# Row maxima kept in PSUM, bias and mask of the first pairs as matmuls, and another order of the pair run, in a fused attention and gated feed-forward kernel

## The chip, the cores and the metric

The kernel runs on one core of a Trainium2 chip. The metric is the device time of one execution in microseconds (us), as the median of several timed runs. Beside the timed runs one execution was taken by the hardware profiler; all rows below come from it.

## The reference

```python
# q, k, v: (8 batches, 8 heads, 576, 64); s: (8, 8, 576)
scores = (1 / sqrt(64)) * q @ k.T
cum    = cumsum(maximum(s, 0), axis=-1)
scores = where(causal, -1e9, scores + minimum(-(cum[:, None] - cum[None, :]), 0))
attn   = exp(scores - max(scores))
attn   = attn / (attn.sum() + 1e-9)
x      = attn @ v                      # heads side by side: (8, 576, 512)
h      = maximum(x @ w_in, 0)          # w_in: (512, 1024), in fp64
conv   = sum(conv_w[k] * h_shifted_by(k - 1) for k in 0, 1, 2)   # along the sequence
out    = (h * sigmoid(conv)) @ w_out   # w_out: (1024, 512), in fp64
```

## The kernel before

Attention runs over 32 pairs: pair p holds two heads, one on partitions 0 to 63 and one on 64 to 127 (the two lanes, j = 0 and 1), with the head dimension on the partitions. Four pairs make a batch. After a batch's four pairs the second layer of that batch follows: `h` (x by w_in), the convolution and the gate, and `o` (u by w_out).

**One pair.** Its keys and queries are loaded (`raw`), and split into a high and a low part for fp32 accuracy (L1014, L1018). The row maxima are needed before the exponential, so TensorE first multiplies the high parts alone, with queries on the partitions: the shift matmuls (L1085, task `sh`). They come in four parts (SH_PARTS): 288 keys of the last query block; its other 288; 448 of block 3 and 64 of block 0; 320 of block 2 and 192 of block 1. Each part takes two PSUM banks, one per lane, and a bank is free again when VectorE has read its maximum. That is L1102, `tensor_tensor_reduce`: it adds to the PSUM block a row of the scaled cumulated bias (`bb`, loaded with the same row on all partitions by a 576 KB DMA, L1045, and masked on the diagonal block by GpSimd's `affine_select`, L1058) and takes the maximum along the row into one column of `r`. It must also write the sum somewhere; here that is one bf16 scrap tile in SBUF, `junk`. On VectorE it shows as two instructions, CUSTOM_DVE_ANT_0 and DVE_READ_ACCUMULATOR2_ANT. A pair has 12 of them.

The maxima are turned (a TensorE transpose, L1126), copied by ScalarE with a base value added (L1134), and sent by DMA into two rows of `eq` (the shift rows, L1142). The score matmuls (L1174, task `sc`), keys on the partitions, are again four parts of two banks: per block three products of high and low parts, and one of `ek` by `eq`, which adds the bias and the shift. `ek` holds nine rows per lane of the bias, loaded by L1028: for pairs 0 and 1 straight from the SBUF tile `bx`, later from a copy in DRAM (`rows_d`). For pairs 0 to 7 the causal mask is added by a bf16 matmul of `unit` and `mask` (L1178); from pair 8 on GpSimd cuts the result (L1209). ScalarE takes the exponential (L1196). Then TensorE adds up rows (L1252, `sum`) and multiplies by the values (L1234, `pv`). The row sums go through a guard, a reciprocal, DRAM and back as `rb`, and the normalization (L1298) and a split (L1313, L1317) give `x`.

**PSUM.** Two of the eight banks hold `pv`; six are handed out to the shift parts, the scores, the sums and the second layer.

**What sets the order.** All work is cut into tasks with the engines on which they may run and an estimated duration. A planner, `Sched.play`, simulates the engines when the kernel is built, and each engine takes, of the tasks that are ready, the one with the smallest due time. Due times stand in a table of numbers, DUE. One rule goes beyond them: from pair 8 (B0) on, the sums and values of the pair before, the scores of this pair and the shift parts of the next form a pair run: on TensorE they follow each other in the fixed order ORDER, with nothing between. All engines then execute their instructions in the order thus found; what waits for another engine waits on its semaphore.

**Weights.** w_in, w_out and conv_w come in fp64 and are put together to fp32 by bit operations on VectorE (L866, L877, L880, L888, tasks `one`, `two`, `three`), a piece at a time. The convolution's two outer taps are two `scalar_tensor_tensor` in one task (L1386).

## Time and profile before

| | before |
|---|---|
| timed runs, median of 3 | 818.46 us (818.03 to 819.22) |
| the profiled execution | 821.87 us |
| its span | 820.2 us |
| TensorE (PE), matmuls | 8437 |
| VectorE (DVE), instructions | 1367 |
| ScalarE (ACT) busy | 437.3 us |
| GpSimd (POOL) busy | 370.9 us |
| DMA | 82.32 MB, mean 100 GB/s |

PE is TensorE's matmuls, PEld its weight loads, which lie beside them; DVE is VectorE, ACT ScalarE, POOL GpSimd, SP SyncE, whose queue (SPq) issues the DMAs. In a row of a timeline the two numbers in front are start and duration in us; a bracket at its end gives the time that the engine stood idle before it and what ended that. "x6" stands for six instructions in one row, which overlap and of which the row gives the whole stretch. PEclk is the granted TensorE clock as a share of the full 2.4 GHz. The stretches in the last section are cut at events: 48.58 us is the start of the first row sums, 111.78 us that of the first matmul of the second layer, 184 us about that of the first pair run, 733 us the end of the last.

### The profile page before, as it was taken

What the parts mean: (1) busy time and instruction counts of PE and PEld (TensorE: products, weight loads), DVE (VectorE), ACT (ScalarE), POOL (GpSimd) and SP (SyncE); (2) the same over time, 40 slices, a digit from 0 to 9 for tenths busy, and PEclk for the clock granted to TensorE, in tenths of its full rate; (3) what the DMA queues carried; (4) which work ended last, traced back from release to release, by engine and by line L of the source; (5) the groups of instructions that cost most, each with busy time, mean ns of one, the idle gap of its engine ahead of it and who ended that gap; (6) DMA issues with size and microseconds to landing.
All of it is one profiled execution on the core that took longest, in us unless ns stands there. A gap on an engine that the chain in (4) does not pass through costs nothing.

```text
span 820.2 us, 21742 instructions
## 1 busy us (share of the span) xinstructions
PE 769.1 (94%) x8437; PEld 685.5 (84%) x8437; DVE 539.6 (66%) x1367; ACT 437.3 (53%) x998; POOL 370.9 (45%) x633
## 2 busy tenths in 40 slices
PE   1498999999999999999999999999899999999998
PEld 1266677898989889898988989898798989899998
DVE  6878989876585756657576655656586566754633
ACT  5345556764573546546564547545454666454543
POOL 8237443355455254636454454546426362513122
PEclk9999999999999999999999999999999999999999
DMA  7836534423314132333223142333303320111001
GB/s 244 272 122 189 159 114 147 154 82 112 102 51 143 55 118 81 110 104 104 88 80 114 64 134 84 103 110 83 111 35 110 109 81 16 51 43 52 16 30 37
DMA packets 59004, 82.32 MB, mean 100 GB/s; under 512 B 6617, under 2 KB 39705, under 8 KB 58841
## 3 DMA queue, kind: packets, MB, share of 16 engines
q1 hardware_dynamic: 58901, 80.94, 31.5%
q8 instruction: 66, 1.08, 0.6%
q14 instruction: 37, 0.30, 0.1%
HBM read 67.48 MB, written 13.19 MB: 98 GB/s over the span
## 4 chain that ended last, share of the span: by engine, by line
PE 72%; DVE 12%; issue 5%; ACT 5%; DMA 3%; POOL 1%; SPq 1%; DVEq 0%; POOLq 0%; ACTq 0%
PE ps L1444 23%; PE ps L1349 21%; PE ps L1174 12%; PE pv L1234 7%; DVE junk L1102 5%; PE ps L1252 4%; DVE ct L1386 3%; PE ps L1085 3%; ACT pt L1196 2%; DVE ct L1405 1%; DMA ek<-bx 1%; DMA raw<-qk 1%; DMA rb<-ri_d 1%; PE ps L1178 1%; DMA w<-w_in 1%
## 5 line engine op out<-in xcount | busy, mean ns | idle before, releaser
L1444 PE MATMUL ps<-u,wo 128*128 128x288 f32 x1536 | 218.3, 298 | 0.5 <-ACT ob L1461 0.5
L1349 PE MATMUL ps<-x,wi 128*128 128x290 f32 x1536 | 215.7, 298 | 0.4 <-ACT pt L1196 0.4
L1349 PEld LDWEIGHTS ps<-x,wi 128*128 128x128 f32 x1536 | 209.2, 190 | 1.6 <-ACT pt L1196 0.6
L1444 PEld LDWEIGHTS ps<-u,wo 128*128 128x128 f32 x1536 | 208.0, 189 | 2.5 <-ACT ob L1461 0.7
L1386 DVE SCALAR_TENSOR_TENSOR ct<-ht,cw_sb,ct 128x288 f32<-128x288 f32 (+1 forms) x256 | 150.0, 589 | 90.0 <-ACT ct L1372 84.5
L1196 ACT ACTIVATE pt<-ps,bias_sb 128x288 f32<-128x288 f32 (+4 forms) x384 | 153.4, 477 | 85.2 <-PE ps L1174 84.7
L1416 POOL TENSOR_TENSOR u<-ct,u 128x576 fp32r<-128x576 f32 x64 | 96.4, 1509 | 212.6 <-ACT u L1412 176.3
L1102 DVE CUSTOM_DVE_ANT_0 junk<-ps,bb 128x64 bf16<-128x64 f32 (+4 forms) x320 | 137.1, 429 | 67.3 <-PE ps L1085 26.7
L1058 POOL TENSOR_SCALAR_AFFINE_SELECT bb<-bb 128x128 f32<-128x128 f32 (+1 forms) x256 | 90.3, 360 | 137.0 <-DVE r L1102 120.5
L1174 PE MATMUL ps<-s 64*128 64x288 f32 (+4 forms) x1152 | 126.5, 316 | 9.1 <-ACT pt L1196 4.3
L1174 PEld LDWEIGHTS ps<-s 64*128 64x128 f32 x1152 | 97.4, 190 | 22.8 <-ACT pt L1196 10.5
L1209 POOL TENSOR_SCALAR_AFFINE_SELECT pt<-pt 128x128 f32<-128x128 f32 (+1 forms) x240 | 79.9, 349 | 48.7 <-ACT pt L1196 47.3
L1360 ACT ACTIVATE ht<-ps 128x289 f32<-128x289 f32 x128 | 52.7, 412 | 84.0 <-PE ps L1349 82.9
L1234 PE MATMUL pv<-pt,v 128*32 128x448 f32 (+4 forms) x1536 | 97.3, 396 | 0.0
L1018 POOL TENSOR_TENSOR s<-raw,s 128x1152 fp32r<-128x1152 f32 x31 | 83.1, 2680 | 23.4 <-DVE s L1014 15.3
L1234 PEld LDWEIGHTS pv<-pt,v 128*32 128x32 f32 x1536 | 63.0, 112 | 29.1 <-issue 24.2
L1085 PE MATMUL ps<-s 64*128 64x288 f32 (+4 forms) x384 | 52.9, 340 | 21.0 <-ACT s L1014 7.9
L1174 PE MATMUL ps<-eq,ek 64*128 64x288 f32 (+4 forms) x384 | 69.2, 322 | 0.9 <-DMA eq<-rt 0.9
L1372 ACT ACTIVATE ct<-ht,cw_sb 128x288 f32<-128x288 f32 x122 | 65.4, 536 | 5.0
L1252 PE MATMUL ps<-pt,onehot 128*32 128x144 f32 (+4 forms) x1792 | 63.8, 278 | 2.1 <-DVE r L1102 1.3
L1252 PEld LDWEIGHTS ps<-pt,onehot 128*32 128x32 f32 x1792 | 56.9, 115 | 9.2 <-issue 3.6
L1085 PEld LDWEIGHTS ps<-s 64*128 64x128 f32 x384 | 33.0, 194 | 36.8 <-DVE r L1102 9.0
(82 smaller groups left out, 594.2 us busy)
## 6 DMA issues: line engine op xcount, KB each, us to landing
raw<-qk SPq DMA_DIRECT2D x32, 576.0 KB
bb<-cum_d SPq DMA_DIRECT2D x32, 576.0 KB
v<-vp SPq DMA_DIRECT2D x32, 320.0 KB
rb<-ri_d SPq DMA_DIRECT2D x64, 144.0 KB
outT<-ob SPq DMA_DIRECT2D x64, 144.0 KB
ht<-w_out SPq DMA_DIRECT2D x16, 256.0 KB
w<-w_in SPq DMA_DIRECT2D x8, 512.0 KB
ri_d<-ri SPq DMA_DIRECT2D x32, 72.0 KB
```

The costliest lines, as they stand in the source:

```text
L1018: tt_on(e)(st[:, 0:2, :], R_t[raw.slot], st[:, 2:4, :].bitcast(F32), op=ALU.subtract)
L1058: nc.gpsimd.affine_select(out=dst, in_=src, pattern=[[0, n], [-1, P if tau else P - PAD]], compare_op=ALU.is_ge, fill=NEG, base=0 if tau e ...
L1085: nc.tensor.matmul(dst[j], l, S_t[sb.slot][r, 2, c0:c1], start=True, stop=True)
L1102: nc.vector.tensor_tensor_reduce(out=junk[:, 0 : c1 - c0], in0=bank(pb, o, o + c1 - c0), in1=in1, scale=1.0, scalar=acc if c0 else -3.0e38 ...
L1174: nc.tensor.matmul(dst[j], l, m, start=(k == 0), stop=(k == 3))
L1196: nc.scalar.activation(PT_t[pts[j].slot][0:jt, O_T[t] + c0 : O_T[t] + c1], bank(pb, o, o + c1 - c0)[0:jt], AF.Sigmoid, bias=bias_sb[0:jt, ...
L1234: nc.tensor.matmul(pvt[gs, o0 : o0 + c1 - c0], vt[0:jt, t, gs], PT_t[pts[g // 2].slot][0:jt, O_T[t] + c0 : O_T[t] + c1], start=(t == 0), s ...
L1252: nc.tensor.matmul(bank(sb_, o0, o0 + b_ - a_)[32 * g : 32 * g + 32], onehot[:, j, :], src[:, a_ - c0 : b_ - c0], start=t == 0 and j == 0, ...
L1349: nc.tensor.matmul(bank(hb, 0, XW), l, r, start=(k == 0), stop=(k == len(seq) - 1))
L1386: nc.vector.scalar_tensor_tensor(cc[:, lo:hi], h_[:, sh + lo : sh + hi], cw_sb[:, 3 * f + k : 3 * f + k + 1], cc[:, lo:hi], op0=ALU.mult, ...
L1416: tt_on(e)(uu[:, 1], C_t[ct.slot], uu[:, 0].bitcast(F32), op=ALU.subtract)
L1444: nc.tensor.matmul(bank(pb, 0, HS), l, r, start=(fp == 0 and k == 0), stop=(fp == NF // 2 - 1 and k == len(seq) - 1),)
```

## The change

- The maxima write the biased block back into the PSUM bank they read (`out=src`) instead of `junk`, and stand in an order that alternates the two lanes. One `affine_select` cuts the `bb` of both lanes.
- For pairs 0 to 5 (B1) the bias is added on TensorE: behind each shift matmul stands one of indicator rows EB by `ek`, and the diagonal blocks but the last get the mask by a matmul of `unit` and `mask` (three blocks wide now). VectorE then takes a plain maximum (`tensor_reduce`) where a row block begins at key 0, ten a pair, and keeps the old form with `mask` as the added tile for the second half of the last block. These pairs load no `bb` and have no cuts; their shift matmuls now need `ek`; their turned maxima are copied by one instruction.
- ORDER is changed, the two taps and the two ORs of a weight piece become tasks of their own, SW replaces the number 0.19 in the planner, and DUE is new throughout.
- On SyncE's queue six `bb` loads go, and the second `bb` load (pair 7's) now stands between the `ek` loads of pairs 0 and 1.

```diff
+B1 = 6
...
+SW = 0.12
...
-ORDER = ("sh0", "sh1", "sh2", "sum", "pv", "sc0", "sh3", "sc1", "sc2", "sc3")
+ORDER = ("sh0", "sum", "pv", "sh1", "sc0", "sh2", "sc1", "sc2", "sh3", "sc3")
...
 DUE = (
-    -114439, -2886, -5304, -2876, -2883, -2878, -5567, -4957, -5119, -16050, -13717, 193, -603,
+    -71591, -3748, -2936, -3146, -2870, -3586, -4314, -2902, -3422, -2825, -6319, -11723, -11558,
...
-                        dur += 0.19
+                        dur += SW
...
-    MW = 2 * P
+    MW = 3 * P
-    junk = const.tile([P, P * (NT - 1) - PAD], BF16, name="junk")
+    EB_t = const.tile([P, FW], F32R, name="eb")
...
+    t_eb = add("eb", [("ACT", 0.72)], [t_masks], -188, c_ind(EB_t))
...
                 nc.vector.scalar_tensor_tensor(
                     wb, wd[:, :, 1], 0xC0000000, wb, op0=ALU.bitwise_and, op1=ALU.bitwise_or
                 )
+
+            def low(e):
+                wd, _, wb = parts()
                 nc.vector.scalar_tensor_tensor(
                     wb, wd[:, :, 0], 29, wb, op0=ALU.logical_shift_right, op1=ALU.bitwise_or
                 )
...
-        last_v[0] = t_v = add(f"v{p}", [("SP", 0.4)], [last_v[0], *t_ind], A - 2, load_v,
+        last_v[0] = t_v = add(f"v{p}", [("SP", 0.4)], [last_v[0], t_eb, *t_ind], A - 2, load_v,
...
-        bb = buf("bb")
+        early = p < B1
+        if not early:
...
+        if not early:
+            t_bb = add(f"bb{p}", [("SP", 0.4)], [t_cum_d], a_sh - BBA, load_bb, alloc=[bb],
+                       nbytes=2 * P * S * 4)
+
+        def cut(tau, deps):
             def run(e):
-                b_ = BB_t[bb.slot][:, j0 : j0 + n]
+                b_ = BB_t[bb.slot]
                 c0 = P * tau - PAD
                 src = b_[:, :, max(c0, 0) : c0 + P]
                 dst = b_[:, :, S : S + P - PAD] if tau == 0 else src
                 nc.gpsimd.affine_select(
-                    out=dst, in_=src, pattern=[[0, n], [-1, P if tau else P - PAD]],
+                    out=dst, in_=src, pattern=[[0, 2], [-1, P if tau else P - PAD]],
                     compare_op=ALU.is_ge, fill=NEG, base=0 if tau else -PAD, channel_multiplier=1,
                 )
 
-            return add(f"{name}{p}.{tau}.{j0}", [("POOL", 0.18 + n * 0.135, True)], deps, a_sh - 1.0,
-                       run, uses=[bb])
-
-        cuts = {}
-        for tau in (L, 0):
-            t_cut = cut("cu", [0, 1], tau, [t_bb])
-            cuts[tau, 0] = cuts[tau, 1] = t_cut
-
+            return add(f"cu{p}.{tau}", [("POOL", 0.42 if tau else 0.3, True)], deps, a_sh - 1.0, run,
+                       uses=[bb])
+
+        cuts = {} if early else {tau: cut(tau, [t_bb]) for tau in (L, 0)}
 
         r8, rt = buf("r8"), buf("rt")
         maxima, last_mx = [], {}
...
                         l = S_t[sb.slot].rearrange("p a c -> p (a c)")[
                             r, 3 * S - PAD + P * tau : 3 * S - PAD + P * tau + P]
                         nc.tensor.matmul(
-                            dst[j], l, S_t[sb.slot][r, 2, c0:c1], start=True, stop=True
+                            dst[j], l, S_t[sb.slot][r, 2, c0:c1], start=True, stop=not early
                         )
+                    if early and tau < L:
+                        dg = min(P, c1)
+                        for j in range(2):
+                            nc.tensor.matmul(
+                                dst[j][:, c1 - dg : c1], unit, mask[:, MW - dg : MW],
+                                start=False, stop=False,
+                            )
+                    if early:
+                        for j, r in enumerate(lanes):
+                            nc.tensor.matmul(
+                                dst[j], EB_t[r, P * tau : P * tau + P],
+                                EK_t[ek.slot][r, c0:c1], start=False, stop=True,
+                            )
                     o += c1 - c0
 
             w = sum(c1 - c0 for _, c0, c1 in part)
-            t_mm = add(f"sh{p}.{i}", [("PE", sum(c_rt(c1 - c0) for _, c0, c1 in part))], [t_hi],
+            t_mm = add(f"sh{p}.{i}", [("PE", (1 + early) * sum(c_rt(c1 - c0) for _, c0, c1 in part)
+                                           + 0.22 * early * sum(tau < L for tau, _, _ in part))],
+                       [t_hi] + ([t_dr, t_eb, t_ident] if early else []),
                        a_sh + 0.1 * i, sh_mm, alloc=pbs + ([r8] if i == 0 else []),
-                       uses=[sb], mode="r", prev=None if p - 1 >= B0 else t_mm,
+                       uses=[sb] + ([ek] if early else []), mode="r", prev=None if p - 1 >= B0 else t_mm,
                        burst=group(p - 1, f"sh{i}"))
             note(p - 1, f"sh{i}", t_mm, [t_hi])
-            for j in range(2):
-                o = 0
-                for tau, c0, c1 in part:
+            o = 0
+            for tau, c0, c1 in part:
+                for j in range(2):
+                    w = c1 - c0
+
                     def sh_max(e, j=j, tau=tau, c0=c0, c1=c1, o=o, pb=pbs[j]):
                         acc = R8_t[r8.slot][:, j * NT + tau : j * NT + tau + 1]
-                        in1 = BB_t[bb.slot][:, j, c0:c1] if tau else BB_t[bb.slot][:, j, S : S + c1]
+                        src = bank(pb, o, o + c1 - c0)
+                        if early and not c0:
+                            nc.vector.tensor_reduce(
+                                out=acc, in_=src, axis=mybir.AxisListType.X, op=ALU.max
+                            )
+                            return
+                        if early:
+                            in1 = mask[:, MW - (c1 - c0) : MW]
+                        elif tau:
+                            in1 = BB_t[bb.slot][:, j, c0:c1]
+                        else:
+                            in1 = BB_t[bb.slot][:, j, S : S + c1]
                         nc.vector.tensor_tensor_reduce(
-                            out=junk[:, 0 : c1 - c0], in0=bank(pb, o, o + c1 - c0),
-                            in1=in1, scale=1.0, scalar=acc if c0 else -3.0e38,
+                            out=src, in0=src, in1=in1, scale=1.0, scalar=acc if c0 else -3.0e38,
                             op0=ALU.add, op1=ALU.max, accum_out=acc,
                         )
 
                     need = [t_mm]
-                    if c1 == P * (tau + 1) - PAD:
-                        if (tau, j) not in cuts:
-                            cuts[tau, j] = cut("cu", [j], tau, [last_mx[tau + 1, j]])
-                        need.append(cuts[tau, j])
+                    if early:
+                        need.append(t_ident)
+                    elif c1 == P * (tau + 1) - PAD:
+                        if tau not in cuts:
+                            cuts[tau] = cut(tau, [last_mx[tau + 1, k] for k in range(2)])
+                        need.append(cuts[tau])
                     else:
                         need.append(t_bb)
                     if c0:
                         need.append(last_mx[tau, j])
                     last_mx[tau, j] = t_mx = add(
-                        f"mx{p}.{j}.{tau}.{c0}", [("DVE", 0.22 + (c1 - c0) / 0.96e3)],
-                        need, a_sh + 0.1 * i, sh_max, uses=[pbs[j], r8, bb],
+                        f"mx{p}.{j}.{tau}.{c0}",
+                        [("DVE", (0.15 if early and not c0 else 0.19) + w / 0.96e3)],
+                        need, a_sh + 0.1 * i, sh_max, uses=[pbs[j], r8] + ([] if early else [bb]),
                     )
                     maxima.append(t_mx)
-                    o += c1 - c0
+                o += c1 - c0
...
                      uses=[r8])
 
         def rt_cp(e):
+            if early:
+                nc.scalar.copy(RT_t[rt.slot], bank(tb, 0, P)[0 : 2 * NT, :])
+                return
             for k in range(2):
                 h = slice(k * BLK, k * BLK + BLK)
                 nc.scalar.activation(
...
-            def tap(e, i=i, f=f):
+            def tap(e, k, i=i, f=f):
...
-            taps.append(add(f"ta{b}.{hf}.{f}", [("DVE", 1.03, True)], [t_c],
-                            h_tag(b, hf, f) + 0.1, tap, uses=[ht, ct]))
...
+            t_k = t_c
+            for k in (0, 2):
+                t_k = add(f"ta{b}.{hf}.{f}.{k}", [("DVE", 0.53, True)], [t_k],
+                          h_tag(b, hf, f) + 0.1, lambda e, k=k, tap=tap: tap(e, k), uses=[ht, ct])
+            taps.append(t_k)
```

How the change moves the instructions is shown at three places. In these rows a name with a number is one buffer of that name (ps_66 is a PSUM bank, s_82 and s_83 the split keys and queries of two pairs), the last figures are the size, and x6 counts equal instructions. The names in brackets are the semaphores that the instruction waits for: DVE_49 is VectorE's own, PE_49 TensorE's, Activation_49 ScalarE's, Pool_49 GpSimd's, a DMAHW one that of a DMA.

VectorE, before, the first maxima of a pair in the long middle; the second row is the accumulator read that follows each maximum, left out afterwards:

```order
L1102 ISA junk,r_100<-ps_66,bb_90 128x288 [waits DMAHW7_49,PE_49]
L1102 ISA r_100 128x1
L1102 ISA junk,r_100<-ps_65,bb_90 128x288 [waits DVE_49]
...
L1102 ISA junk,r_100<-ps_70,bb_90 128x64 [waits DVE_49,PE_49,Pool_49]
...
L1102 ISA junk,r_100<-ps_68,bb_90 128x64 [waits DVE_49,Activation_49]
...
L1102 ISA junk,r_100<-ps_69,bb_90,r_100 128x288 [waits DVE_49]
...
L1102 ISA junk,r_100<-ps_67,bb_90,r_100 128x288 [waits DVE_49]
```

VectorE, the change, the first maxima of a pair at the same place of the program:

```order
L1422 SCALAR_TENSOR_TENSOR ct_111<-ht_106,cw_sb,ct_111 128x288 [waits Activation_49]
L1134 ISA ps_65,r_100<-ps_65,bb_91 128x288 [waits DMAHW4_49,PE_49]
L1134 ISA r_100 128x1
L1134 ISA ps_67,r_100<-ps_67,bb_91 128x288 [waits PE_49]
...
L1422 SCALAR_TENSOR_TENSOR ct_111<-ht_106,cw_sb,ct_111 128x288 [waits Activation_49]
L1422 SCALAR_TENSOR_TENSOR ct_111<-ht_106,cw_sb,ct_111 128x287 [waits DVE_49] x2
L1313 RECIPROCAL ri<-rs 128x144 [waits DMAHW6_49,Activation_49]
L1444 TENSOR_TENSOR ct_111<-ct_111,ht_106 128x576 [waits Activation_49]
L1134 ISA ps_66,r_100<-ps_66,bb_91,r_100 128x288 [waits PE_49]
...
L1134 ISA ps_65,r_100<-ps_65,bb_91,r_100 128x288
...
L1134 ISA ps_69,r_100<-ps_69,bb_91 128x64 [waits PE_49]
...
L1134 ISA ps_69,r_100<-ps_69,bb_91 128x448 [waits DVE_49,Pool_49]
```

Five of the six maxima shown of before carry DVE_49, besides what else they wait for. In the change only the last one, which needs a cut behind two other maxima, carries it, and taps of the convolution (L1422), a reciprocal (L1313) and a product (L1444) stand between the maxima of the first part and those of the second.

TensorE, before, the start of a pair run: o matmuls, three shift parts of the next pair (s_82), and then the row sums of the pair before:

```order
L1444 MATMUL ps_65<-u_1144,wo 128x288 x6
L1085 MATMUL ps_66<-s_82 128x288
L1085 MATMUL ps_67<-s_82 128x288
L1085 MATMUL ps_68<-s_82 128x288
L1085 MATMUL ps_69<-s_82 128x288
L1085 MATMUL ps_65<-s_82 128x448
L1085 MATMUL ps_70<-s_82 128x448
L1085 MATMUL ps_65<-s_82 128x64
L1085 MATMUL ps_70<-s_82 128x64
L1252 MATMUL ps_66<-pt_95,onehot 32x144 x4
L1252 MATMUL ps_66<-pt_96,onehot 32x144 x4
```

TensorE, the change, the start of a pair run (first fence), and the rows of the same run from the last value matmul on (second):

```order
L1386 MATMUL ps_66<-x,wi 128x290 x12
L1089 MATMUL ps_65<-s_83 128x288
L1089 MATMUL ps_67<-s_83 128x288
L1289 MATMUL ps_68<-pt_95,onehot 32x144 x4
L1289 MATMUL ps_68<-pt_96,onehot 32x144 x4
L1289 MATMUL ps_68<-pt_95,onehot 32x16
```

```order
L1271 MATMUL pv<-pt_96,v_93 32x64 x2
L1089 MATMUL ps_65<-s_83 128x288
L1089 MATMUL ps_66<-s_83 128x288
L1211 MATMUL ps_67<-s_82 128x288
L1211 MATMUL ps_68<-s_82 128x288
...
L1211 MATMUL ps_67<-eq_87,ek_85 128x288
L1211 MATMUL ps_68<-eq_87,ek_85 128x288
L1089 MATMUL ps_69<-s_83 128x448
L1089 MATMUL ps_70<-s_83 128x448
L1089 MATMUL ps_69<-s_83 128x64
L1089 MATMUL ps_70<-s_83 128x64
L1211 MATMUL ps_65<-s_82 128x288
```

One shift part (s_83) instead of three stands ahead of the sums; the second stands behind the values, the third between the first score part (ps_67 and ps_68) and the second.

TensorE, before, the start of the program: the turn of pair 0 (r_100), the last shift part of pair 1 (s_83), the turn of pair 1 (r_101) and the first scores of pair 0 (s_82):

```order
L1085 MATMUL ps_66<-s_83 128x64
L1085 MATMUL ps_67<-s_83 128x64
L1126 MATMUL ps_68<-ident,r_100 128x128
L1085 MATMUL ps_69<-s_83 128x320
L1085 MATMUL ps_70<-s_83 128x320
L1085 MATMUL ps_69<-s_83 128x192
L1085 MATMUL ps_70<-s_83 128x192
L1126 MATMUL ps_65<-ident,r_101 128x128
L1174 MATMUL ps_65<-s_82 128x288
L1174 MATMUL ps_66<-s_82 128x288
```

TensorE, the change, the same place from the turn of pair 0 on, the first shift part of pair 1 and then the end of its third part and the first scores of pair 0 (L1101 is the bias matmul, L1095 the mask):

```order
L1160 MATMUL ps_65<-ident,r_100 128x128
L1089 MATMUL ps_65<-s_83 128x288
L1089 MATMUL ps_66<-s_83 128x288
L1101 MATMUL ps_65<-ek_85,eb 128x288
L1101 MATMUL ps_66<-ek_85,eb 128x288
...
L1089 MATMUL ps_69<-s_83 128x64
L1089 MATMUL ps_70<-s_83 128x64
L1095 LDWEIGHTS unit
L1095 MATMUL ps_69<-mask,unit 128x64
...
L1101 MATMUL ps_69<-ek_85,eb 128x64
L1101 MATMUL ps_70<-ek_85,eb 128x64
L1211 MATMUL ps_65<-s_82 128x288
L1211 MATMUL ps_66<-s_82 128x288
```

The scores of pair 0 now stand behind three shift parts of pair 1 with their bias and mask, and ahead of its last part and its turn.

## Rows read from the trace of the kernel before

**Rows 1.** The page's busy table: busy us (share of span) xinstructions.

```profile
PE 769.1 (94%) x8437; PEld 685.5 (84%) x8437; DVE 539.6 (66%) x1367; ACT 437.3 (53%) x998; POOL 370.9 (45%) x633
```

**Rows 2.** Windows by stage: us, PE, PEld, DVE, ACT, POOL busy, PEclk, DMA share, GB/s.

```profile
48.58:111.78 63.20, 58.38 (x813) 42.65 (x809) 54.39 (x154) 30.42 (x78) 33.93 (x46) 0.95 0.55 172
111.78:184.00 72.22, 70.40 (x699) 60.78 (x697) 62.86 (x163) 48.05 (x114) 28.97 (x38) 1.00 0.38 119
184.00:733.00 549.00, 536.81 (x6060) 488.89 (x6059) 347.56 (x890) 295.75 (x681) 264.05 (x479) 1.00 0.29 90
733.00:820.20 87.20, 83.41 (x779) 80.15 (x777) 40.35 (x62) 41.43 (x85) 19.39 (x21) 1.00 0.10 32
```

**Rows 3.** Groups by line, TensorE, 184 to 733 us: busy, mean ns, idle before.

```profile
L1174 PE MATMUL ps<-s 64*128 64x288 f32 (+4 forms) x828 | 90.1, 312 | 6.3 <-DVE r L1102 3.2 <-ACT pt L1196 2.7
...
L1252 PE MATMUL ps<-pt,onehot 128*32 128x144 f32 (+3 forms) x1288 | 42.8, 267 | 1.6 <-DVE r L1102 1.3
L1085 PE MATMUL ps<-s 64*128 64x288 f32 (+4 forms) x276 | 33.8, 319 | 4.2 <-ACT ob L1461 2.1 <-DVE r L1102 1.1 <-ACT ht L1360 0.4
```

**Rows 4.** Timeline, TensorE, one pair run: start, us, instruction [idle before].

```profile
617.79 0.67 PE L1174 MATMUL ps<-s 64*128 64x288 f32 x6 [0.38 <-DVE r L1102]
...
621.48 0.71 PE L1174 MATMUL ps<-s 64*128 64x320 f32 x6 [0.44 <-DVE r L1102]
```

**Rows 5.** Timeline, VectorE, two maxima and a weight operation.

```profile
49.70 0.08 DVE L1102 DVE_READ_ACCUMULATOR2_ANT r<- 128x1 f32 x1
...
49.92 0.23 DVE L1102 CUSTOM_DVE_ANT_0 junk<-ps,bb 128x64 bf16<-128x64 f32 x1
...
50.07 0.09 DVE L1102 DVE_READ_ACCUMULATOR2_ANT r<- 128x1 f32 x1
50.07 1.44 DVE L866 TENSOR_SCALAR w<-w 128x512 uint32<-128x512 uint32 x1
```

**Rows 6.** Timeline, TensorE, scores with mask (87 us) and without (447 us).

```profile
87.30 0.41 PE L1174 MATMUL ps<-s 64*128 64x64 f32 x6
...
87.94 0.69 PE L1174 MATMUL ps<-s 64*128 64x320 f32 x6
...
89.02 0.47 PE L1174 MATMUL ps<-s 64*128 64x192 f32 x6
...
89.93 0.33 PE L1126 MATMUL ps<-ident,r 128*128 128x128 f32 x1
...
447.37 0.42 PE L1174 MATMUL ps<-s 64*128 64x64 f32 x6
...
447.74 0.68 PE L1174 MATMUL ps<-s 64*128 64x320 f32 x6
448.25 0.31 PE L1174 MATMUL ps<-eq,ek 64*128 64x320 f32 x2
448.40 0.48 PE L1174 MATMUL ps<-s 64*128 64x192 f32 x6
...
448.92 0.33 PE L1126 MATMUL ps<-ident,r 128*128 128x128 f32 x1
```

**Rows 7.** Windows, TensorE alone: us, PE busy, PEclk, DMA share, GB/s.

```profile
16.00:18.00 2.00, 0.13 (x1) 1.00 0.37 103
64.00:66.00 2.00, 2.00 (x42) 0.50 0.01 3
```

**Rows 8.** Timeline of the start, all engines.

```profile
15.30 1.73 SPq L1028 DMA_DIRECT2D ek<-bx  x2
...
32.95 0.47 PE L1126 MATMUL ps<-ident,r 128*128 128x128 f32 x1 [3.96 <-DVE r L1102]
...
34.02 1.09 PE L1174 MATMUL ps<-s 64*128 64x288 f32 x6 [0.59 <-ACT rt L1134]
...
36.37 0.61 PE L1174 MATMUL ps<-eq,ek 64*128 64x288 f32 x2 [0.94 <-DMA eq<-rt]
```

**Rows 9.** The chain that ended last: start, us, step.

```profile
20.93 7.45 DMA ek<-bx
```

More of the change, by code (lines that the diff above doesn't have):

```diff
@@ L896, in weight_piece @@
             t1 = add(name + "1", [("DVE", 0.13 + n / 1.6e3, True)], [t0], tag, one, uses=ws)
-            t2 = add(name + "2", [("DVE", 2 * c_tt(n) + 0.1, True)], [t1], tag, two, uses=ws)
-            last = add(name + "3", [("DVE", c_tt(n) + 0.05, True)], [t2, ta], tag, three, uses=ws)
+            t2 = add(name + "2", [("DVE", c_tt(n), True)], [t1], tag, two, uses=ws)
+            t3 = add(name + "4", [("DVE", c_tt(n), True)], [t2], tag, low, uses=ws)
+            last = add(name + "3", [("DVE", c_tt(n), True)], [t3, ta], tag, three, uses=ws)
         def hi(e):
@@ L1377, in moe_h @@
                       [t_relu, t_cw], h_tag(b, hf, f) + 0.1, center, uses=[ht, ct])
-            def tap(e, i=i, f=f):
+            def tap(e, k, i=i, f=f):
                 h_ = H_t[ht.slot][:, i, :]
                 cc = C_t[ct.slot][:, i, :]
-                for k in (0, 2):
-                    sh = hf + k - 1
-                    lo = 1 if sh < 0 else 0
-                    hi = HS - 1 if sh + HS > HS + 1 else HS
-                    nc.vector.scalar_tensor_tensor(
-                        cc[:, lo:hi], h_[:, sh + lo : sh + hi],
-                        cw_sb[:, 3 * f + k : 3 * f + k + 1], cc[:, lo:hi],
-                        op0=ALU.mult, op1=ALU.add,
-                    )
-            taps.append(add(f"ta{b}.{hf}.{f}", [("DVE", 1.03, True)], [t_c],
-                            h_tag(b, hf, f) + 0.1, tap, uses=[ht, ct]))
+                sh = hf + k - 1
+                lo = 1 if sh < 0 else 0
+                hi = HS - 1 if sh + HS > HS + 1 else HS
+                nc.vector.scalar_tensor_tensor(
+                    cc[:, lo:hi], h_[:, sh + lo : sh + hi],
+                    cw_sb[:, 3 * f + k : 3 * f + k + 1], cc[:, lo:hi],
+                    op0=ALU.mult, op1=ALU.add,
+                )
+            t_k = t_c
[3 more added lines that the diff above has]
+            taps.append(t_k)
         tg = h_tag(b, hf, 2 * fp + 1) + 0.2
```

7 lines of the change are left out of this document (2 added, 5 removed), and 452 rows, old and new, of the table DUE.

## The prediction

> **What bounds the kernel now.** I read the busy table of the page first: TensorE is busy 769.1 of 820.2 us, the next engine, VectorE, 539.6 [rows 1]. Then the stretches between landmarks of the order [rows 2]: from the first row-sum step (48.58 us) to the first matmul of the second layer (111.78 us) TensorE lacks 63.20 - 58.38 = 4.8 us, then 1.8 us up to 184 us, 12.2 us in the long middle where one attention pair follows the other between matmuls of the second layer (184 to 733 us), and 3.8 us in the tail. The remaining idle time, 820.2 - 769.1 - 22.6 = 28.5 us, lies before 48.58 us. So TensorE is the bound from about 49 us on. Time can come from the start, from the 12.2 us of the pair runs, or from less TensorE work; this change adds TensorE work. In the middle the groups by line say what ended the idle time [rows 3]: score matmuls wait 3.2 us for VectorE's maxima and 2.7 us for ScalarE, the sums 1.3 us and the shift matmuls 1.1 us for maxima. One run shows the shape [rows 4]: 0.38 us before the first score part, 0.44 us before the last, both for a maximum that still held a bank.
>
> **Own PSUM banks for the maxima.** All 384 maxima of before write one scrap tile, junk, and the order shows what that costs: 328 of them wait for VectorE's own semaphore. With such a wait the next maximum starts 0.22 us after the start of the accumulator read (49.70 to 49.92); an instruction without it starts together with that read (50.07 and 50.07) [rows 5]. Afterwards 324 maxima of this kind are left (60 became plain reductions), and in the piece of order shown the plain ones wait for TensorE alone. Of 12 maxima in a pair about 9 lose the wait: 9 x 0.2 = 2 us of VectorE per pair. Writing fp32 to PSUM instead of bf16 to SBUF is not in the trace. The nearest rows are the 64-wide maximum, 0.23 us [rows 5], and nothing that writes PSUM from VectorE; I take no change, and as bounds 0.1 us less and 0.2 us more for each of 12, 1.2 us less to 2.4 us more a pair. VectorE is not the bound in the middle (347.56 of 549 us [rows 2]), so only what it holds back from TensorE counts, which is the next term.
>
> The Trainium skill (VectorE: DVE Perf Modes, The DRAIN you can't avoid) says that a semaphore between chained VectorE instructions costs nothing extra, since the pipe drains anyway. By that rule this edit is worth 0 and only the new order acts. The trace disagrees, with 0.22 us against 0.00 us above; I go by the trace.
>
> **New order in the pair run.** Before, three shift parts (six banks, all there are) stand ahead of the sums, so the sums wait for the first maximum and the first score part for later ones. After, one shift part stands ahead of the sums and the others between score parts. While sums and value matmuls run, VectorE then has two maxima instead of eight to do. The waits ahead of the sums and of the first score part should go; splitting the tap pairs into single tasks helps the same way, since a maximum can now slip between two taps. What is late next: the second score part needs two banks, which the two maxima of the second shift part must free. At 0.5 us each they fit about into the matmuls between. Bounds: all 12.2 us [rows 2] come back, or 3 us more are lost. I take two thirds, -8.2.
>
> **Bias and mask on TensorE in the first six pairs.** Each pair gets 12 bias matmuls (six pairs of two half-array ones) and 8 mask matmuls (four steps of two full-array ones). The same two kinds stand in the score parts. The mask: from the 64-wide score group to the next it takes 87.94 - 87.30 = 0.64 us with a mask step and 447.74 - 447.37 = 0.37 us without, so 0.27; 320 wide 1.08 against 0.66, so 0.42; 192 wide 0.91 against 0.52, so 0.39 [rows 6]. With the 448 wide one taken as 0.42, four steps are 1.50 us. A bias pair at 320 is 448.40 - 448.25 = 0.15 us [rows 6]; six are 0.90. Together 2.40 us per pair, 14.4 us for six. Pairs 0 and 1 and the first two parts of pair 2 (0.3) stand ahead of the first sums in the new order, as their shift matmuls did before, and belong to the start. After it come 2.1 + 3 x 2.40 = 9.3 us, on a TensorE with little idle time: +9.3.
>
> Against it: VectorE does ten plain reductions per pair without accumulator read or own wait, the selections on GpSimd and the 576 KB broadcast loads go, and the copy of the turned maxima is one instruction instead of two. These lie beside TensorE; they count where it waited, 4.8 + 1.8 us before 184 us [rows 2]. Many of these waits are for ScalarE's exponentials, and more matmuls in front give it time. The granted clock also reads 0.50 (the 1.2 GHz level) in 64 to 66 us [rows 7], after a stretch with waits; fewer waits may spare one such fall. I take -4 of it all (bounds 0 and -8).
>
> **The start.** Before, the first score matmul stands behind both pairs' turned maxima. TensorE waits 3.96 us for pair 1's, starts at 34.02 us and waits again until 36.37 us for the shift rows [rows 8]. After, the scores of pair 0 stand ahead of pair 1's last shift part and of its turn, so that wait goes. A new one comes: the shift parts now read ek. Pair 0's rows are issued at 15.30 us [rows 8], and from 16 to 18 us the transfers nearly run dry (0.37 busy [rows 7]), so I estimate 18 us for their landing. Twelve maxima of about 0.5 us follow, and the turn comes near 25.5 us. But pair 1's rows land 7.45 us after 20.93, at 28.4 us [rows 9], and a 576 KB load now stands between the two ek loads on the queue (pair 7's bb): 28.4 to 30.5 us. Behind it pair 1's three first parts take about 4 us at the low speed of the start, so the scores of pair 0 begin at 32 to 34.5 us, with the shift rows already there. Before they began at 34.02 and lost 0.94 us to the shift rows [rows 8], as if at 35.0: 0.5 to 3 us later. Pair 1's last part and pair 2's first two, longer by about 1.5 us at low speed, take that back; but TensorE no longer stands still for 3.96 and 0.94 us, and may reach its full speed before the first sums instead of after them. I take -1.5 (bounds -5 and +4).
>
> Weight ORs as single tasks, the wider mask memset and the extra copy of the indicator rows lie beside the wait for ek and cost nothing; without that cover 0.3 us on GpSimd and 0.7 us on ScalarE. The tail keeps its back-to-back matmuls: 0.
>
> **Sum.** -1.5 + 9.3 - 4 - 8.2 = -4.4 us on the profiled 821.87 us (820.2 span and 1.7 around it): 817.5. The median of the three timed runs, 818.46 us, is 3.4 us lower; the same difference puts it at 814.1, and I say 814.
>
> **Rivals.** (a) The wait moves instead of going, and the kernel gets slower. In the new run the shift parts two and three and the first score part hold all six banks; if VectorE is in a reciprocal or a product when the second shift part ends, the second score part waits a microsecond. For it: waits for maxima already stand before score parts [rows 4]. Against: eight of the maxima no longer crowd behind the sums, and each is 0.2 us shorter. With 23 such runs, waits of 0.66 us per run (15.2 us) instead of 0.53 turn -8.2 into +3, the total into +6.8: 825. The others sum to +3.8, so the kernel is slower as soon as the runs give back less than that: from 8.4 us of waits, 0.37 per run, on. (b) The start decides: ek lands 3 us later, VectorE is idle until then, and the 9.3 us stand in full, with nothing absorbed: +1.5 + 9.3 - 8.2 = +2.6, 821. For it: all of pair 1 hangs on one transfer. (c) The wait for VectorE's own semaphore only covers a pause that stays without it; the maxima get no cheaper, and the new order alone returns a third, -4: 814 + 4.2 = 818. Against it: the 0.22 us and 0.00 us side by side [rows 5]. This is what the rule of the Trainium skill quoted above (VectorE: DVE Perf Modes) would do here. (d) All goes well: the middle loses 11 us of waits, the first stretch absorbs 6, the start gives 3: -1.5 - 2 - 2.8 = -6.3 on top of 814, 808.
>
> **Chances.** The forecast 0.47 (its own range 809 to 818), (a) 0.15, (b) 0.12, (c) 0.12, (d) 0.14. Less than 0.2%, 1.6 us, can't be told from no change. Faster takes most of the forecast (0.38), all of (d) and some of (c), 0.57; same takes parts of forecast, (b) and (c), 0.14; slower 0.29. The range to 8 in 10: 804 to 826.
>
> **What would show it.** Right: the groups by line of 184 to 733 us give the score and sum matmuls under half of their waits for VectorE; the time from an accumulator read to the next maximum falls to under 0.1 us; bias and mask matmuls of pairs 2 to 5 come to 2.4 us a pair; the first sums start near 47 us, the first second-layer matmul later than before in its order. Wrong: maxima that write PSUM lasting 0.1 us longer each, a wait of half a microsecond at every second score part, first scores after 36 us, or more stretches at the low clock.

## The result and the profile after

The changed kernel takes 804.69 us (median of 4 runs, 803.21 to 809.6; before 818.25 us in the same series), a ratio of 0.9845 with a 95% interval of 0.9801 to 0.9889. A second series gave 805.39 us and 0.9855 (0.983 to 0.988). The forecast was 814. The direction held, and the range to 8 in 10 (804 to 826) held by 0.7 us; the time lies below the forecast's own range of 809 to 818, and the size did not hold (-4.4 us were summed up, some -13 came). The profiled execution took 809.6 us; the one of the second series, 805.72 us with a span of 804.0. Two runs, one of e2 (1814 us) and one of e3 (4018 us), took far longer than the others of their kernels and are left out of the medians below.

The page after, its span and busy table (before: [rows 1]):

```profile
span 807.9 us, 21422 instructions
PE 774.9 (96%) x8557; PEld 690.7 (85%) x8557; DVE 544.8 (67%) x1310; ACT 439.5 (54%) x989; POOL 328.7 (41%) x508
```

TensorE does 120 matmuls more, is busy 5.8 us longer, and the span is 12.3 us shorter. Where that happens is seen in windows cut at the same work of both kernels: the first row sums, the sums of pair 7, those of pair 31, the end. First the kernel before, then the changed one (columns as in [rows 2]):

```profile
0.00:48.58 48.58, 20.10 (x98) 12.98 (x98) 34.43 (x100) 21.66 (x43) 24.53 (x51) 1.00 0.72 222
48.58:185.16 136.58, 129.90 (x1518) 104.03 (x1514) 117.87 (x319) 79.33 (x193) 64.06 (x84) 0.98 0.46 144
185.16:747.16 562.00, 549.73 (x6248) 500.61 (x6244) 355.53 (x900) 303.91 (x700) 269.02 (x491) 1.00 0.28 88
747.16:820.20 73.04, 69.37 (x585) 67.84 (x584) 31.77 (x50) 32.41 (x64) 13.26 (x9) 1.00 0.09 31
```

```profile
0.00:43.06 43.06, 24.18 (x137) 16.19 (x137) 31.51 (x74) 20.19 (x40) 19.82 (x36) 1.00 0.68 211
43.06:189.22 146.16, 140.87 (x1589) 107.83 (x1588) 116.00 (x284) 78.85 (x186) 46.69 (x41) 0.96 0.39 121
189.22:733.78 544.56, 539.30 (x6245) 497.90 (x6243) 365.27 (x901) 307.07 (x698) 246.07 (x422) 1.00 0.29 91
733.78:807.90 74.12, 70.50 (x591) 68.79 (x590) 32.05 (x54) 33.41 (x67) 16.09 (x11) 1.00 0.10 32
```

The start wins 5.5 us, the stretch of the early pairs loses 9.6, the middle wins 17.4, and the tail loses 1.1 with six matmuls more in it. In the middle the busy time falls by 10.4 us for practically the same matmuls (6248 and 6245). So the idle time of the rows was not all that TensorE lost there. Part of it is the clock. Once in the middle of before TensorE stood idle for 2.13 us and then ran at the 1.2 GHz level (granted clock 0.50 from 579.2 to 582.5 us, 0.64 in the window below): the row sums took 2.56 us and the values 3.72, where pair 12 below has 1.77 and 2.87. That is 1.6 of the 10.4 us; in the middle of the change no such fall stands in the trace.

```profile
577.34 0.81 PE L1085 MATMUL ps<-s 64*128 64x288 f32 x8 [2.13 <-ACT ob L1461]
578.39 2.56 PE L1252 MATMUL ps<-pt,onehot 128*32 128x144 f32 x54 [0.25 <-DVE r L1102]
...
580.84 3.72 PE L1234 MATMUL pv<-pt,v 128*32 128x128 f32 x46
```

```profile
578.00:582.00 4.00, 3.75 (x74) 0.64 0.23 78
```

The groups by line of the middle after, TensorE (scores, sums, shift matmuls; before: [rows 3]):

```profile
L1211 PE MATMUL ps<-s 64*128 64x288 f32 (+4 forms) x864 | 89.7, 302 | 4.8 <-DVE r L1134 4.2
...
L1289 PE MATMUL ps<-pt,onehot 128*32 128x144 f32 (+4 forms) x1344 | 43.8, 264 | 0.0
L1089 PE MATMUL ps<-s 64*128 64x288 f32 (+4 forms) x276 | 39.5, 331 | 0.0
```

The waits ahead of sums and shift matmuls are gone, and so are those of the scores for ScalarE; what is left (4.2 us for maxima) stands ahead of the second score part, where the prediction had put it. It is more than the 3.2 us for which scores waited for maxima before. The same pair run, that of pair 12, in the timeline of TensorE, before and after:

```profile
277.17 1.13 PE L1085 MATMUL ps<-s 64*128 64x288 f32 x8
279.09 1.77 PE L1252 MATMUL ps<-pt,onehot 128*32 128x144 f32 x54 [0.80 <-DVE r L1102]
...
285.73 1.26 PE L1174 MATMUL ps<-s 64*128 64x448 f32 x6 [0.60 <-ACT pt L1196]
...
288.90 0.67 PE L1444 MATMUL ps<-u,wo 128*128 128x288 f32 x3
```

```profile
280.22 0.40 PE L1089 MATMUL ps<-s 64*128 64x288 f32 x2
280.55 1.77 PE L1289 MATMUL ps<-pt,onehot 128*32 128x144 f32 x54
...
286.55 0.66 PE L1211 MATMUL ps<-s 64*128 64x288 f32 x6 [0.39 <-DVE r L1134]
...
287.18 0.77 PE L1211 MATMUL ps<-s 64*128 64x448 f32 x6
...
289.81 0.93 PE L1483 MATMUL ps<-u,wo 128*128 128x288 f32 x5
```

The run takes 288.90 - 277.17 = 11.73 us before and 9.59 after. Of the 2.14 us only 0.80 + 0.60 - 0.39 = 1.01 stand in brackets. Half a microsecond hides in one row: the six 448-wide score matmuls last 1.26 us before and 0.77 after. They are the same six; before, the second of them, which writes the second bank, started 0.39 us after the first, behind a wait for ScalarE of its own, and the row counts that as busy. After, the two start together.

Measured in this way, from the first shift matmul to the first matmul behind the last score or shift part, the 23 runs of pairs 8 to 30 last (us):

| kernel | mean | median | shortest, longest |
|---|---|---|---|
| before | 10.28 | 10.29 | 9.67, 11.73 |
| write-back alone (e1) | 9.92 | 9.90 | 9.70, 10.81 |
| change without write-back (e2) | 9.92 | 9.87 | 9.68, 10.23 |
| write-back and new ORDER alone (e5) | 10.00 | 9.68 | 9.55, 11.38 |
| change with the old ORDER (e6) | 9.99 | 9.86 | 9.76, 11.23 |
| change with taps in pairs (e10) | 9.74 | 9.66 | 9.55, 10.33 |
| the change, both profiles | 9.64 | 9.59 | 9.54, 9.92 |
| change with four scrap tiles (e9) | 9.56 | 9.53 | 9.47, 9.75 |

23 x (10.28 - 9.64) = 14.7 us; with the 2.13 us that TensorE stood idle ahead of one run before (the one with the fall of the clock), 16.8 of the 17.4 us are in the runs.

The idle time that is left in the middle tells what each part took away. By the groups by line of each kernel's middle, in us:

| kernel | order | waits for maxima | waits for ScalarE |
|---|---|---|---|
| before | old | 5.6 | 5.2 |
| write-back alone (e1) | old | 1.5 | 3.1 |
| change with the old ORDER (e6) | old | 0.5 | 3.4 |
| write-back and new ORDER alone (e5) | new | 7.9 | 1.8 |
| change without write-back (e2) | new | 8.5 | 0 |
| the change | new | 4.2 | 0.3 |

The write-back takes away waits for maxima under either order (before to e1, e2 to the change). The new order takes away waits for ScalarE (e1 to e5, e6 to the change), and more waits for maxima stand in their place, nearly all ahead of score matmuls. The rows of the score matmuls of e6 and of e2 show both ends:

```profile
L1274 PE MATMUL ps<-s 64*128 64x288 f32 (+4 forms) x864 | 93.9, 313 | 2.8 <-ACT pt L1296 2.6
```

```profile
L1212 PE MATMUL ps<-s 64*128 64x288 f32 (+4 forms) x864 | 92.4, 306 | 8.8 <-DVE r L1135 8.5
```

### The profile page after: what moved, and what is told of

It is laid out like the page before. It is cut to its first block, busy times and chain, and to the rows that moved or that the text cites. A ratio compares the mean times of both kernels' runs of the same rounds, so it can differ in the third digit from the quotient of the medians.

```text
span 807.9 us, 21422 instructions
## 1 busy us (share of the span) xinstructions
PE 774.9 (96%) x8557; PEld 690.7 (85%) x8557; DVE 544.8 (67%) x1310; ACT 439.5 (54%) x989; POOL 328.7 (41%) x508
## 4 chain that ended last, share of the span: by engine, by line
PE 90%; DVE 4%; ACT 3%; DMA 1%; issue 1%; POOL 0%; SPq 0%; ACTq 0%; DVEq 0%; POOLq 0%
PE ps L1483 26%; PE ps L1386 25%; PE ps L1211 15%; PE pv L1271 11%; PE ps L1289 7%; PE ps L1089 4%; DVE ps L1134 2%; DMA ek<-bx 1%; PE ps L1101 1%; PE ps L1215 1%; ACT pt L1233 1%; PE ps L1095 1%; PE ps L1160 0%; ACT bx L784 0%; DVE ct L880 0%
## 5 line engine op out<-in xcount | busy, mean ns | idle before, releaser
L1422 DVE SCALAR_TENSOR_TENSOR ct<-ht,cw_sb,ct 128x288 f32<-128x288 f32 (+1 forms) x256 | 154.6, 617 | 84.7 <-ACT ct L1409 81.2
L1455 POOL TENSOR_TENSOR u<-ct,u 128x576 fp32r<-128x576 f32 x64 | 94.2, 1477 | 234.2 <-ACT u L1451 201.0
L1134 DVE CUSTOM_DVE_ANT_0 ps<-ps,bb 128x288 f32<-128x288 f32 (+2 forms) x260 | 108.3, 454 | 60.0 <-PE ps L1089 30.6
L1211 PE MATMUL ps<-s 64*128 64x288 f32 (+4 forms) x1152 | 122.8, 309 | 5.7 <-DVE r L1134 4.2
L1066 POOL TENSOR_SCALAR_AFFINE_SELECT bb<-bb 128x256 f32<-128x256 f32 (+1 forms) x130 | 59.4, 466 | 129.5 <-DVE r L1134 102.3
L1211 PEld LDWEIGHTS ps<-s 64*128 64x128 f32 x1152 | 98.3, 190 | 15.7 <-DVE r L1134 10.0
L1271 PEld LDWEIGHTS pv<-pt,v 128*32 128x32 f32 x1536 | 60.0, 111 | 33.0 <-issue 26.2
L1246 POOL TENSOR_SCALAR_AFFINE_SELECT pt<-pt 128x128 f32<-128x128 f32 (+1 forms) x240 | 67.7, 302 | 22.0 <-ACT pt L1233 20.4
L1089 PE MATMUL ps<-s 64*128 64x288 f32 (+4 forms) x384 | 61.9, 345 | 3.7 <-DVE r L1134 1.8
L1289 PE MATMUL ps<-pt,onehot 128*32 128x144 f32 (+4 forms) x1792 | 61.4, 273 | 0.2 <-ACT pt L1233 0.2
L1438 ACT ACTIVATE ct<-ct 128x576 f32<-128x576 f32 x64 | 43.5, 680 | 31.4 <-DVE ct L1422 30.6
```

Of the source, the lines that this page charges most:

```text
L1089: nc.tensor.matmul(dst[j], l, S_t[sb.slot][r, 2, c0:c1], start=True, stop=not early)
L1134: nc.vector.tensor_tensor_reduce(out=src, in0=src, in1=in1, scale=1.0, scalar=acc if c0 else -3.0e38, op0=ALU.add, op1=ALU.max, accum_out=acc,
L1211: nc.tensor.matmul(dst[j], l, m, start=(k == 0), stop=(k == 3))
L1246: nc.gpsimd.affine_select(out=reg, in_=reg, pattern=[[1, dg]], compare_op=ALU.is_ge, fill=0.0, base=0, channel_multiplier=-1,)
L1271: nc.tensor.matmul(pvt[gs, o0 : o0 + c1 - c0], vt[0:jt, t, gs], PT_t[pts[g // 2].slot][0:jt, O_T[t] + c0 : O_T[t] + c1], start=(t == 0), s ...
L1289: nc.tensor.matmul(bank(sb_, o0, o0 + b_ - a_)[32 * g : 32 * g + 32], onehot[:, j, :], src[:, a_ - c0 : b_ - c0], start=t == 0 and j == 0, ...
```

## The experiments

**e1, write-back alone.** The kernel before, orders unchanged:

```diff
-                            out=junk[:, 0 : c1 - c0], in0=bank(pb, o, o + c1 - c0),
+                            out=bank(pb, o, o + c1 - c0), in0=bank(pb, o, o + c1 - c0),
```

> The kernel before, but with each maximum's sum written back to its own PSUM bank in place of junk; every engine's order as in the kernel before. Theory O (the new order of the pair run is what saves time in the middle; the write-back is a small help): 815 to 818 us, the pair runs still 10.0 to 10.3 us long on average. Theory W (the maxima without VectorE's own wait free the banks earlier, and that is what shortens the pair runs whatever the order): 804 to 810 us, pair runs of 9.7 us.

Measured: 810.17 us, ratio 0.9897 (0.9879 to 0.9916), runs 9.92 us, the middle 552.1 us long. The time is at the edge of what W expects, the runs lie between both.

**e2, the change without it.** The changed kernel, orders unchanged, all maxima to one scrap tile:

```diff
-                            out=src, in0=src, in1=in1, scale=1.0, scalar=acc if c0 else -3.0e38,
+                            out=junk[:, 0 : c1 - c0], in0=src, in1=in1, scale=1.0, scalar=acc if c0 else -3.0e38,
```

> The changed kernel, but all maxima write the scrap tile junk again (bf16 in SBUF); every engine's order as in the changed kernel. Theory O: 805 to 808 us, the pair runs stay at 9.6 to 9.8 us. Theory W: 813 to 819 us, the pair runs back at 10.1 to 10.3 us.

Measured: 816.77 us, 0.9976 (0.9956 to 0.9997), runs 9.92 us, the middle 552.15 us. The profiled execution of it took 814.0, 8.3 more than that of the changed kernel's second series. What the others of its runs lost beyond that, no trace shows. Neither theory holds by itself: the write-back gives 0.36 us a run under the old order and 0.28 under the new, the rest gives as much.

**e9, what the write-back takes away.** The changed kernel, orders unchanged, four bf16 scrap tiles in turn:

```diff
-                            out=src, in0=src, in1=in1, scale=1.0, scalar=acc if c0 else -3.0e38,
+                            out=scrap(c1 - c0), in0=src, in1=in1, scale=1.0, scalar=acc if c0 else -3.0e38,
```

> The changed kernel, but the maxima write four bf16 scrap tiles in SBUF in turn instead of their PSUM banks; orders unchanged. A maximum then need not wait for the one just before it, though it still writes SBUF. Theory V (what one scrap tile costs is the wait for the maximum before): pair runs of 9.6 to 9.65 us and 804 to 807 us, as the changed kernel. Theory M (what costs is where it writes): pair runs of 9.9 us and 815 to 818 us, as e2.

Measured: 805.68 us, 0.9869 (0.9833 to 0.9905), runs 9.56 us. Theory V. The timeline of VectorE shows the step from one maximum to the next in one scrap tile (e2), in PSUM (the change), and in four tiles (e9):

```profile
609.08 0.08 DVE L1135 DVE_READ_ACCUMULATOR2_ANT r<- 128x1 f32 x1
609.31 0.52 DVE L1135 CUSTOM_DVE_ANT_0 junk<-ps,bb,r 128x288 bf16<-128x288 f32 x1
```

```profile
606.83 0.14 DVE L1134 DVE_READ_ACCUMULATOR2_ANT r<- 128x1 f32 x1
606.83 0.52 DVE L1134 CUSTOM_DVE_ANT_0 ps<-ps,bb,r 128x288 f32<-128x288 f32 x1
```

```profile
601.45 0.08 DVE L1140 DVE_READ_ACCUMULATOR2_ANT r<- 128x1 f32 x1
601.45 0.52 DVE L1140 CUSTOM_DVE_ANT_0 junk<-ps,bb,r 128x288 bf16<-128x288 f32 x1
```

0.23 us with the wait for the maximum just before, nothing in the other two. In the step of e2 a wait for another engine stands beside VectorE's own; where its own is the only one, the step is 0.12 us (89 of them in the trace of e2, against 96 of 0.23). Where the maxima write matters little, and PSUM is the slower place: a 64-wide maximum took 259 ns there and 219 in SBUF, a 448-wide one 647 and 620, the accumulator read 140 and 83, in the means of all of each form.

**e5, the new order without the rest.** The kernel before with e1's edit and the new ORDER. As the due times fit one order only, DUE was made anew by a search with the kernel's own planner.

```diff
-ORDER = ("sh0", "sh1", "sh2", "sum", "pv", "sc0", "sh3", "sc1", "sc2", "sc3")
+ORDER = ("sh0", "sum", "pv", "sh1", "sc0", "sh2", "sc1", "sc2", "sh3", "sc3")
```

> The kernel before with the write-back to PSUM (as in e1) and the new ORDER of the pair run, nothing else of the change; DUE made anew for this order. Theory P (of what e1 leaves, the new order is the rest: 9.92 to 9.64 us per run): pair runs of 9.6 to 9.7 us, 23 runs by 0.28 less than e1, so 810 - 6.5 = 803 to 805 us. Theory Q (single taps, alternating lanes and joined cuts are the rest, the order does nothing): pair runs still 9.9 us, 809 to 812 us.

Measured: 810.21 us, 0.9894 (0.9873 to 0.9915). The median run is 9.68 us and the shortest 9.55, as P expects, but six of 23 last over 10.3 us and the mean is 10.00. The time is what Q expects. Inconclusive: the new order reaches the short run, and here not every time; whether double taps or its table lets some runs grow, this run can't tell. What the alternating lanes, the joined cuts and the single ORs give was not tried alone.

**e6, the change with the old order.** The two lines of e5's diff the other way round in the changed kernel, DUE made anew.

> The changed kernel with the old ORDER of the pair run, all other parts kept; DUE made anew for this order. Theory P: pair runs back at 9.9 us, 805 + 6.5 = 811 to 813 us. Theory Q: pair runs stay at 9.6 to 9.7 us, 804 to 807 us.

Measured: 808.87 us, 0.9873 (0.9838 to 0.9907); runs 9.99 us, the middle 552.3 us against 544.56. In the middle P holds, with 7.7 us for the order; 2.6 of them are two runs of 11.1 and 11.2 us, which its own table may have made. The total lies between the two, since its table brings the sums of pair 7 forward to 177.6 us.

**e10, taps in pairs.** Both taps issued where the first single one stands, the rest in its order:

```diff
-                          h_tag(b, hf, f) + 0.1, lambda e, k=k, tap=tap: tap(e, k), uses=[ht, ct])
+                          h_tag(b, hf, f) + 0.1, lambda e, k=k, tap=tap: (tap(e, 0), tap(e, 2)) if k == 0 else None, uses=[ht, ct])
```

> The changed kernel with both taps issued where the first of the two single tasks stands; all else in its order. Theory P (order and write-back are all): pair runs within 0.03 us of 9.64, 805 to 806 us. Theory Q (single taps let maxima in between): pair runs of 9.75 us or more, 808 us or more.

Measured: 808.96 us, 0.9887 (0.9871 to 0.9904), runs 9.74 us, the middle 546.9 us. Nearer to Q: the second tap pushes a maximum back in some runs (that of pair 26 goes from 9.68 to 10.33 us), worth 2.3 us in the middle.

**e3, bias and mask left out for pairs 2 to 5.** The same test stands ahead of the mask:

```diff
+        on_pe = early and p < 2
...
-                    if early:
+                    if on_pe:
                         for j, r in enumerate(lanes):
```

> The changed kernel without the bias and mask matmuls of the maxima of pairs 2 to 5 (their maxima are taken of the bare products, so this part of the computation is left out); the order of all else unchanged. Theory F (these matmuls stand in full on TensorE's path, nothing absorbs them): 4 pairs by 2.4 us less, 9.6 us, so 795 us. Theory A (part of them fills waits of TensorE, which come back when they go): 3 to 6 us less, 799 to 802 us.

Measured: 798.99 us (796.01 to 801.84 in three runs), 0.9762 (0.9734 to 0.9791): some 6 us less than the change, nearer to theory A than to F. The stretch from the first sums to those of pair 7 is 140.27 us long with 75 matmuls fewer, against 144.69 in the second profile of the change: 4.4 us less, which is A. The granted clock says part of the why (windows of 4 us, TensorE: us, busy, clock, DMA share, GB/s). The change, then e3, those under 0.9:

```profile
92.00:96.00 4.00, 3.01 (x28) 0.76 0.48 166
96.00:100.00 4.00, 4.00 (x54) 0.81 0.16 34
...
108.00:112.00 4.00, 4.00 (x36) 0.50 0.60 213
112.00:116.00 4.00, 4.00 (x72) 0.68 0.02 4
```

```profile
48.00:52.00 4.00, 2.52 (x18) 0.73 0.87 270
52.00:56.00 4.00, 3.81 (x35) 0.85 0.33 109
68.00:72.00 4.00, 2.43 (x25) 0.79 0.43 141
72.00:76.00 4.00, 4.00 (x73) 0.79 0.40 123
100.00:104.00 4.00, 4.00 (x75) 0.63 0.54 181
128.00:132.00 4.00, 4.00 (x27) 0.54 0.66 227
132.00:136.00 4.00, 4.00 (x22) 0.61 0.14 36
```

Without the added matmuls TensorE waits (2.52 and 2.43 of 4 us busy) and then runs below full clock, in four places instead of two. The matmuls cost less than their duration, most likely because they stood partly in such waits.

**e7 and e8, fewer pairs with bias on TensorE.** DUE made anew for the pairs that load `bb` again; e8 has 3 for the 0 of e7:

```diff
-B1 = 6
+B1 = 0
```

> The changed kernel with B1 = 0: no pair has bias and mask of its maxima on TensorE, all load bb; DUE of the first pairs made anew. Theory S (the start is faster because the maxima of pairs 0 and 1 need no bb and its cuts; the later pairs pay for it): first sums at 46 to 49 us as before, and 136 to 138 us from there to the sums of pair 7 instead of 145, in all 804 to 807 us: the part is worth nothing in sum. Theory N (the start is faster by its new order alone): first sums at 41 to 43 us also here, 796 to 799 us.

> The changed kernel with B1 = 3: pairs 0 to 2 keep bias and mask on TensorE, pairs 3 to 5 load bb again. Theory S: first sums at 41 to 43 us, and three pairs by 1.2 us less (e3 gave back 5 us for four pairs), so 800 to 803 us. Theory N: the matmuls of three pairs go and nothing comes back, 7 us less, 798 us.

Measured: e7 805.08 us, 0.9844 (0.9811 to 0.9877); e8 805.13 us, 0.9833 (0.9815 to 0.9852). In e7 the first sums come late, behind a turn that waits for maxima (timeline of TensorE):

```profile
37.90 0.45 PE L1226 MATMUL ps<-ident,r 128*128 128x128 f32 x1 [10.71 <-DVE r L1200]
...
50.71 3.23 PE L1355 MATMUL ps<-pt,onehot 128*32 128x144 f32 x54
```

From there to pair 7's sums it takes 133.2 us instead of 146.16 and 144.69. So S, for e7: what the bias on TensorE gives the start, 7.7 to 10 us, the change loses in the early pairs, and in sum nothing can be measured. Not all of that loss need be the matmuls: e7's stretch has no time below full clock, the change's has 10.2 us at 0.50, by estimate worth 5 us. e8, which S had put at 800 to 803, keeps half of each and gains nothing. Its first sums come at 45.1 us, not at 41 to 43.

**e4, e11, e12, repeat and tables.** e4 is the change again; e11 has another DUE; e12 joins e9's tiles and e11's table.

> The changed kernel once more, to narrow its time: every theory expects 803 to 806 us and pair runs of 9.6 us.

> The changed kernel with another DUE: the first pairs by the table of e6, the rest searched anew; the same parts, all orders a little different. If the parts make the time and the table little: pair runs of 9.6 to 9.75 us, 802 to 807 us. If the table is worth as much as a part: outside that by 5 us or more.

> The changed kernel with the four scrap tiles of e9 and the table of e11, the two that did best in their stretches: pair runs 0.08 us shorter than in e11 (9.67 us on average), the middle 545 us, the sums of pair 7 at 181 us, and 801 to 804 us. If the gain of e9 were an accident of its table, pair runs of 9.75 us and 805 us.

Measured: e4 805.39 us, with every run as long as in the first profile to within 0.02 us. e11 805.02 us, 0.9832 (0.9807 to 0.9858), runs 9.75 us: in the total, the parts make the time and not the table. By stretches the table does count: with as many matmuls in each, e11's early pairs take 139.98 us instead of 144.69, its middle 546.86 instead of 544.56. e12 802.82 us (799.51 to 807.79), 0.9801 (0.9767 to 0.9834), runs 9.64 us; the sums of pair 7 come at 185.0 us, not at 181. That is the lowest median of the kernels that leave nothing out, but its interval overlaps that of the change, so faster than before is shown, faster than the change is not.

## Why the prediction was right in direction and wrong in size

The profiled span fell by 12.3 us: -5.5 in the start, where -1.5 was taken, +9.6 in the early pairs (+9.3 - 4 = +5.3), -17.4 in the middle (-8.2) and +1.1 in the tail (0). That the first two misses, -4.0 and +4.3, cancel is luck: with the start's alone the time would have been about 800 us, below the range to 8 in 10. Rival (d), 808, came nearest in time, but by other terms: it had the early pairs absorb 6 us and the middle give 11.

**The maxima's own wait: right.** 0.22 us per maximum was read from [rows 5], and e2 and e9 show it as the step that vanishes. It holds where a wait for another engine stands beside (158 steps of before, 0.23 us); 71 others with VectorE's own wait alone took 0.12. The Trainium skill (VectorE: DVE Perf Modes, The DRAIN you can't avoid) measured no difference between eight copies with a semaphore after each and with one after the last, and has the semaphore cost nothing extra. For these maxima e2 against e9 shows otherwise, with 0.23 us against 0.00 a step, and some 8 us in all (e1's median, e2's profile). The bounds for writing PSUM held too: 0.01 to 0.04 us more each.

**The new order: the term mis-sized, -8.2 for -17.4, and its wait only partly the right one.** The step that failed is "Bounds: all 12.2 us [rows 2] come back, or 3 us more are lost". It took the idle time of the rows for all that the runs could give. A row counts a matmul as running while its neighbours wait, so waits of half a row's length are busy time. Taken end to end, 23 runs of 10.28 us against the shortest of before, 9.67, held 14 us, and that could have been read ahead.

The waits that went are not the ones it named. Those ahead of the sums did go (1.3 us), but scores and sums together wait 4.2 us for maxima after 4.5, so the sign "under half of their waits for VectorE" did not come. What the order took away of the idle time were waits for ScalarE, 1.3 us (e1 to e5) and 3.1 us (e6 to the change); why ScalarE comes too late in the old order stays open.

Undone one by one, the write-back gives 7.6 us of the middle (e2), the order 7.7 (e6) and the single taps 2.3 (e10), together 17.6. That this comes near 17.4 does not show that the parts add: the write-back alone, on the old kernel, gives 9.9 (e1). By median runs the order is worth 0.22 us a run (e1 to e5) and 0.27 (e6 to the change), 5 to 6 us in all; another table alone moved the median by 0.10 (e11).

**What is late next: right.** The second score part, with 4.2 us of waits for maxima in all, 0.18 us a run. Rival (a) had it at 0.66 and fell; rival (c), the maxima no cheaper, falls with e9.

**Bias and mask: price right, absorption wrong in this table.** 2.40 us a pair were summed up. The groups by line of 43 to 189 us after (bias, mask) hold:

```profile
L1101 PE MATMUL ps<-ek,eb 64*128 64x288 f32 (+4 forms) x45 | 9.5, 394 | 0.0
...
L1095 PE MATMUL ps<-mask,unit 128*128 128x128 bf16 (+1 forms) x32 | 4.6, 230 | 0.0
```

These overlap others; counted from each matmul's start to the next one's, idle time left out, they add 6.3 + 3.5 = 9.8 us there, against 9.3 forecast. But the stretch grew by 9.6 (8.1 in the second profile), so at most 1.5 of the -4 us came back in the sum. The clock fell twice again, later. That is rival (b)'s full price, without its late start.

With other tables the same matmuls cost less. With them the stretch takes 139.98 us in e11, 141.16 in e12 and 138.35 in e6 (seven more in it), only 1.8 to 4.6 us longer than the 136.58 of before, though the first sums come as early (40.94, 43.80 and 39.25 us). So most of the price can be absorbed; e3, 4.4 us shorter without 9.8 us of matmuls, says so too. What in the change's order of the early pairs takes it back stays open; the clock does not account for it, since e11's stretch has as much time at 0.50 as the change's (10.2 us).

**The start: right mechanism, mis-sized, -1.5 for -5.5 and -7.9, outside its bound of -5.** In the timeline of TensorE after:

```profile
16.88 0.60 PE L1101 MATMUL ps<-ek,eb 64*128 64x288 f32 x1 [3.05 <-DMA ek<-bx]
...
26.91 0.77 PE L1101 MATMUL ps<-ek,eb 64*128 64x288 f32 x2 [0.75 <-DMA ek<-bx]
...
29.97 1.07 PE L1211 MATMUL ps<-s 64*128 64x288 f32 x6
...
43.06 3.33 PE L1289 MATMUL ps<-pt,onehot 128*32 128x144 f32 x56
```

The waits for pair 0's `ek` ended at 16.88 and 17.82 us and that for pair 1's at 26.91, earlier than the 18 and 28.4 to 30.5 us assumed; the loads were issued at 14.23 and 17.44 us instead of 15.30 and 18.88; the scores began at 29.97 instead of 32 to 34.5 us. In this profile TensorE waited for nothing from there to the first sums. In the second profile the matmuls reached their full speed at about 35 us (two 128-wide mask matmuls take 0.40 us at 34.28 and 0.29 at 36.59), before the first sums at 40.67, as the last clause of that step had left open. In the first profile it was only at about 46 us, behind the sums, which took 3.33 us for 56 matmuls there and 1.83 in the second; the start won 5.5 us all the same.
